# Grouped-query attention and a gated unit on one core: gate with tokens on partitions, and the projection moved behind the next batch's first tiles

## The chip, the cores and the metric

The kernel runs on one core of a Trainium2 chip. The core has five engines that run their own instruction queues in order: TensorE (PE, with weight loads shown apart as PEld), VectorE (DVE), ScalarE (ACT), GpSimd (POOL) and SyncE (SP), which here issues nearly all transfers. The transfers of a core run on 16 DMA engines. The metric is the device time of one execution in microseconds (us). Before the change it is 260.7 us, the median of three runs (259.04 to 261.53).

## The reference

Eight batches of attention with 16 query heads over 4 key and value heads (384 tokens, head size 64), then a gated unit over the 1,024 joined columns. Inputs and output are float32; the kernel works in float16 with float32 sums.

```python
scores = scale * np.matmul(q, k.transpose(0, 1, 3, 2))
attn = np.exp(scores - max); attn = attn / sum
x = (attn @ v), heads joined: (B, 384, 1024)
h = np.maximum(x @ w_in, 0.0)                 # w_in 1024 x 1024
u, v = h[..., :512], h[..., 512:]
v_n = (v - mean(v)) / np.sqrt(var(v) + 1e-06) # over the 512 columns of a token
v_s = np.einsum('ts,bsd->btd', w_spatial, v_n) + b_spatial[None, :, None]
out = (u * v_s) @ w_out                       # w_out 512 x 1024
```

## The kernel before

The order of instructions is written out by hand. One loop of 150 steps `n` makes the program; a batch has 18 steps (`NU`), one for each of its 6 groups `m` (query tile `qt`, head half `j`) times 3 key tiles.

In a step the loop first runs what `at(n, ...)` has put on its list (loads, casts, transposing transfers), then, at even `n`, `scores` for two steps (four matmuls with 64 rows of contraction, and one exponential of 128x1024 on ACT for each step), then `weigh` for a group whose three exponentials came before (12 matmuls of 65 columns, a reciprocal and a product on DVE that write a part of `x16`), then transposes on PE that `turn_at` has put there, and last `run_fill`: as many matmuls of the gated unit as the step is owed, counted in columns. PE runs exactly this order. So attention of one batch and the gated unit of the batch before it are interleaved.

`x16` has the tokens on partitions; the gated unit needs it turned (`xt`, columns on partitions). In batch 0, and for the last third of batch 7, PE does that. Otherwise SP issues transposing transfers, `x_turn`: the first third (`qt` 0) in step 18b+8, the second in step 18b+14, the last in two pieces in steps 18b+17 and 18b+20. k and q of the later batches are turned in the same way, by `k_turn` and `q_turn` (L226 and L233) in steps 10 and 12 of the batch before. Raw k, q and v of a batch are loaded (in step 11 of two batches earlier) and cast on POOL. All of these stand in one queue on SP, in the order of the steps: first x piece, `k_turn`, `q_turn` 0, four loads, `q_turn` 1, second x piece, and so on. At the end of each output tile SP also issues its write to HBM.

`gated_unit(b)` (L306) is a generator that yields the columns of each matmul. `pv` (L314): three token tiles, each 8 matmuls of 512 columns; then relu, mean and variance on DVE. `pu` (L336): four column tiles m of u, transposed (columns on partitions, 384 tokens in the free direction), 8 matmuls of 384 each; relu on ACT. In between, the inverse deviation on ACT, and the normalised `vn` on POOL (L354). `psp` (L366, L369): for each of the four column tiles one matmul that adds the bias to an empty accumulator (a row of ones times a row of bias) and three that mix the tokens; DVE multiplies by u into `gT` (L377). `po` (L384): for each token tile two halves of four matmuls with 512 columns; DVE and ACT copy a half each (L393), SP writes the tile (L397).

The unit of batch b starts in step 18(b+1)+2 and is spread over 18 steps; that of batch 0 starts in step 13. A unit has 43,008 columns, so a step gets 2,389 (2,048 for the first unit, some of which is done early). The accumulators of the unit share three PSUM buffers (`ps_ck`). The rest of batch 7's unit comes after the last attention step, and PE runs it alone.

Of the kernel before, what the change touches and what calls it, by code (L numbers as in the profile page):

```python
# [9 lines left out]
FP32 = mybir.dt.float32  # L10
FP16 = mybir.dt.float16
AF = mybir.ActivationFunctionType
ALU = mybir.AluOpType
# [4 lines left out]
def kernel(  # L18
# [16 lines left out]
    nc = tc.nc  # L35
    P = 128
    B, HQ, S, D = q.shape
# [3 lines left out]
    DH = DFF // 2  # L41
# [14 lines left out]
    att = ctx.enter_context(tc.tile_pool(name="att", bufs=2))  # L56
    moe = ctx.enter_context(tc.tile_pool(name="moe", bufs=2))
    small = ctx.enter_context(tc.tile_pool(name="small", bufs=4))
    ops = ctx.enter_context(tc.tile_pool(name="ops", bufs=4))
    ps_sc = ctx.enter_context(tc.tile_pool(name="ps_sc", bufs=2, space=PSUM))  # L60
    ps_av = ctx.enter_context(tc.tile_pool(name="ps_av", bufs=1, space=PSUM))
    ps_ck = ctx.enter_context(tc.tile_pool(name="ps_ck", bufs=3, space=PSUM))
# [92 lines left out]
    v1 = [cst.tile([P, HKV, NT, VW], FP16, name=f"v1_{i}") for i in range(2)]  # L155
    for i in range(2):
        nc.gpsimd.memset(v1[i][:, :, :, D:VW], 1.0)
    ones_b = cst.tile([P, P], FP16, name="ones_b")
    nc.gpsimd.memset(ones_b, 0.0)
    nc.gpsimd.memset(ones_b[0:1, :], 1.0)  # L160
    nc.gpsimd.memset(ones_b[32:33, :], 1.0)
    bias_b = cst.tile([P, S], FP16, name="bias_b")
    nc.gpsimd.memset(bias_b, 0.0)


    k16s, q16s = {}, {}
# [118 lines left out]
    def x_tile(b):  # L285
        if b not in xts:
            xts[b] = att.tile([P, NT, NB, P], FP16, name=f"xt_{b}", tag="xt")
        return xts[b]
# [13 lines left out]
        )  # L302

    def gated_unit(b):  # L306
        xt = x_tile(b)
        last = b == B - 1
        mv = small.tile([P, NT, 2], FP32, name=f"mv_{b}", tag="mv")
        v_r, v_n = [], []  # L310
        for st in range(NT):
            pv = ps_ck.tile([P, 512], FP32, name=f"pv_{b}_{st}", tag="ck")
            for kt in range(NB):
                nc.tensor.matmul(  # L314
                    pv,
                    xt[:, st, kt],
                    w_in16[:, kt, DH:DFF],
                    start=(kt == 0),
                    stop=(kt == NB - 1),
                )  # L320
                if kt < NB - 1:
                    yield 512
            vr = moe.tile([P, DH], FP32, name=f"vr_{b}_{st}", tag="vr", bufs=4)
            nc.vector.tensor_scalar(vr, pv, 0.0, None, op0=ALU.max)  # L324
            stats = small.tile([P, 6], FP32, name=f"stats_{b}_{st}", tag="stats")
            nc.vector.bn_stats(stats, vr)  # L326
            nc.vector.bn_aggr(mv[:, st, :], stats)
            v_r.append(vr)
            yield 512
        rstd = small.tile([P, NT], FP32, name=f"rstd_{b}", tag="rstd")  # L330
        nmr = small.tile([P, NT], FP32, name=f"nmr_{b}", tag="nmr")
        uT = moe.tile([P, NM, S], FP16, name=f"uT_{b}", tag="uT")
        for m in range(NM):
            pu = ps_ck.tile([P, 512], FP32, name=f"pu_{b}_{m}", tag="ck")
            for kt in range(NB):
                nc.tensor.matmul(  # L336
                    pu[:, 0:S].rearrange("p (t s) -> p t s", t=NT),
                    w_in16[:, kt, m * P : (m + 1) * P],
                    xt[:, :, kt],
                    start=(kt == 0),  # L340
                    stop=(kt == NB - 1),
                )
                yield S
            nc.scalar.activation(uT[:, m, :], pu[:, 0:S], AF.Relu)  # L344
            if m == 0:
                nc.scalar.activation(rstd, mv[:, :, 1], AF.Ln, bias=eps_t)
                nc.scalar.activation(rstd, rstd, AF.Exp, scale=-0.5)
            if m == 1:
                nc.vector.scalar_tensor_tensor(  # L349
                    nmr, mv[:, :, 0], -1.0, rstd, op0=ALU.mult, op1=ALU.mult  # L350
                )
                for st in range(NT):
                    vn = moe.tile([P, DH], FP16, name=f"vn_{b}_{st}", tag="vn", bufs=6)
                    nc.gpsimd.tensor_scalar(  # L354
                        vn,
                        v_r[st],
                        rstd[:, st : st + 1],
                        nmr[:, st : st + 1],
                        op0=ALU.mult,
                        op1=ALU.add,  # L360
                    )
                    v_n.append(vn)
        gT = moe.tile([P, NM, S], FP16, name=f"gT_{b}", tag="gT")
        for m in range(NM):
            psp = ps_ck.tile([P, 512], FP32, name=f"psp_{b}_{m}", tag="ck")
            nc.tensor.matmul(psp[:, 0:S], ones_b, bias_b, start=True, stop=False)  # L366
            yield S
            for st in range(NT):
                nc.tensor.matmul(  # L369
                    psp[:, 0:S],  # L370
                    v_n[st][:, m * P : (m + 1) * P],
                    wsT16[:, st, :],
                    start=False,
                    stop=(st == NT - 1),
                )
                yield S
            nc.vector.tensor_tensor(gT[:, m, :], psp[:, 0:S], uT[:, m, :], ALU.mult)  # L377
        rows = out[b].rearrange("(p t) d -> p t d", t=NT)
        for tt in range(NT):
            osb = ops.tile([P, DM], FP32, name=f"osb_{b}_{tt}", tag="osb")  # L380
            for half in range(2):
                po = ps_ck.tile([P, 512], FP32, name=f"po_{b}_{tt}_{half}", tag="ck")
                for m in range(NM):
                    nc.tensor.matmul(  # L384
                        po,
                        gT[:, m, tt * P : (tt + 1) * P],
                        w_out16[:, m, half * 512 : (half + 1) * 512],
                        start=(m == 0),
                        stop=(m == NM - 1),
                    )  # L390
                    yield 512
                cols = slice(half * 512, (half + 1) * 512)
                (nc.scalar.copy if half else nc.vector.tensor_copy)(osb[:, cols], po)  # L393
                if last:
                    nc.sync.dma_start(rows[:, tt, cols], osb[:, cols])
            if not last:
                nc.sync.dma_start(rows[:, tt, :], osb)  # L397

    HV = NB * 512
    COLS = NT * HV + NM * NB * S + NM * (NT + 1) * S + NT * 2 * NM * 512  # L400


    b32 = cst.tile([1, S], FP32, name="b32")

    def load_b():
        nc.sync.dma_start(b32, moe_b_spatial.rearrange("(a s) -> a s", a=1))

    def prep_spatial():
        lo32 = cst.tile([1, S], FP32, name="lo32")
        bp = b32.rearrange("a (p t) -> a t p", t=NT)  # L410
        hi = bias_b[0:1, :].rearrange("a (t p) -> a t p", t=NT)
        nc.gpsimd.tensor_copy(hi, bp)
        nc.gpsimd.tensor_tensor(lo32.rearrange("a (t p) -> a t p", t=NT), bp, hi, ALU.subtract)
        nc.gpsimd.tensor_copy(bias_b[32:33, :], lo32)

    def load_ws():
        t = cst.tile([P, NT, S], FP32, name="ws32")
# [19 lines left out]
    def at(n, f, *args):  # L437
        todo.setdefault(n, []).append((f, args))
# [64 lines left out]
    at(19, load_q, 2, 1)  # L503
    at(19, load_v, 2)
    at(20, cast_ws)
    at(20, prep_spatial)
    for st in range(NT):
        turn_at(24 + st, ws_transposes, st)
    for c in range(2):
# [22 lines left out]
            elif m > 3:  # L532
                at(s0 + 3 * m + 5, x_turn, b, 2, 4 * (m - 4), 4 * (m - 3))

    fill = []
    owed = 0.0
    total = NU * B

    def run_fill(cols):
        nonlocal owed  # L540
        owed = owed + cols if fill else 0.0
        while fill and owed > 0:
            try:
                owed -= next(fill[0])
            except StopIteration:
                fill.pop(0)

    early = 0
    for n in range(total + 6):
        for f, args in todo.pop(n, []):  # L550
            f(*args)
        if n + 1 < NU:
            scores(n + 1)
        elif n >= NU and n % 2 == 0 and n < total:
            scores(n)
            scores(n + 1)
        for hh in range(2):
            b, r = divmod(n - 3 - hh, NU)
            if n >= 3 + hh and r % 3 == 0 and b < B:
                weigh(b, r // 3, hh)  # L560
        for f, args in turns.pop(n, []):
            f(*args)
        if n == 13:
            fill.append(gated_unit(0))
        if n >= 2 * NU + 2 and (n - 2) % NU == 0 and (n - 2) // NU <= B:
            fill.append(gated_unit((n - 2) // NU - 1))
        if n < NU + 3:
            if 13 <= n and early < 2 * HV:
                c = min(768, 2 * HV - early)
                early += c  # L570
                run_fill(c)
        else:
            run_fill((COLS - (early if n < 2 * NU + 2 else 0)) / (NU if n >= 2 * NU + 2 else NU - 1))
    for g in fill:
        for _ in g:
            pass
    assert not todo and not turns
# [1 line left out]
_INS = ['q', 'k', 'v', 'moe_w_in', 'moe_w_spatial', 'moe_b_spatial', 'moe_w_out']  # L579
# [26 lines left out]
```

## Time and profile before

| what | us |
|---|---|
| median of three runs | 260.7 |
| the profiled execution, its own time | 262.4 |
| its span (first to last instruction) | 260.3 |
| PE busy | 246.5 |
| ACT busy | 169.3 |
| DVE busy | 140.7 |
| POOL busy | 72.8 |
| mean share of the DMA engines, main queue | 72.6% of the span |
| mean granted clock of PE | 0.967 |

The page gives, for each group of equal instructions, the engine, the operation, output and inputs, the count, the busy time, the mean duration of one, and the idle time just before them with what ended it. A matmul's duration is its time in flight, and neighbours overlap. The chain of waits follows the last instruction back to what released it; lines like "87.29 0.54 PE sc L252 x4" in it give start, length and what ran. The list of SP's queue gives the start and the time that SP was held by an instruction; a transfer's landing is counted from its issue. A batch takes 28.5 us in the middle of the run: the first `pv` of the units starts at 65.64, 94.11, 124.02, 152.53, 181.01 and 209.60 us.

### The profile page before, as it was taken

Reading aid. Unit: us, or ns where it says so; the run is one execution under the profiler, and the core shown is the slowest. Engines: PE = TensorE matmul, PEld = TensorE weight load, DVE = VectorE, ACT = ScalarE, POOL = GpSimd, SP = SyncE. Lnnn points to the kernel's source line nnn. Section 1 sums busy time; section 2 is a strip of 40 time slices with the busy share of each in tenths; the row PEclk is TensorE's granted clock in tenths of the full one; section 3 lists DMA queues with packets and bytes.
Section 4 is the critical chain, followed back from the end, with each engine's and each line's share of the span. In section 5 each row is a group of like instructions: output and inputs, shape, how many; then the busy total and the mean of one; then the engine's idle time right before and its main releaser. Section 6 shows DMA issues by size and latency. Waiting matters only on the chain.

```text
span 260.3 us, 5771 instructions
## 1 busy us (share of the span) xinstructions
PE 246.5 (95%) x2339; PEld 126.3 (49%) x2339; DVE 140.7 (54%) x368; ACT 169.3 (65%) x219; POOL 72.8 (28%) x112
## 2 busy tenths in 40 slices
PE   6789889999999999998999999999999999999994
PEld 6445445554455444553455444554455445545551
DVE  3336678355664557274564557274755467364642
ACT  3857556777677776868477776868677776861221
POOL 2455799433003510316003610333021000300110
PEclk9755999999999999999999999999999999999999
DMA  7999798899529991899748991799549350126006
GB/s 189 330 354 353 278 387 263 147 324 224 189 38 197 305 288 52 108 280 209 287 39 195 309 309 33 147 329 232 176 79 134 114 191 14 29 40 241 3 0 242
DMA packets 78827, 49.84 MB, mean 191 GB/s; under 512 B 48081, under 2 KB 72658, under 8 KB 78802
## 3 DMA queue, kind: packets, MB, share of 16 engines
q1 hardware_dynamic: 77762, 49.23, 72.6%
q8 instruction: 18, 0.29, 0.5%
q10 hardware_dynamic: 1040, 0.26, 0.4%
q14 instruction: 7, 0.06, 0.1%
HBM read 25.76 MB, written 12.58 MB: 147 GB/s over the span
## 4 chain that ended last, share of the span: by engine, by line
PE 89%; DVE 5%; ACT 3%; issue 1%; POOL 0%; DVEq 0%; POOLq 0%
PE av L266 16%; PE pu L336 16%; PE pv L314 16%; PE sc L252 15%; PE po L384 15%; PE psp L369 6%; ACT aT L259 2%; PE psp L366 2%; DVE x L278 2%; PE warm L453 1%; DVE qT L224 1%; ACT osb L393 1%; DVE r L276 1%; DVE gT L377 1%; PE qps L217 1%
## 5 line engine op out<-in xcount | busy, mean ns | idle before, releaser
L259 ACT ACTIVATE aT<-sc 128x1024 f16<-128x1024 f32 x144 | 139.9, 1023 | 62.4 <-PE sc L252 62.4
L266 PEld LDWEIGHTS <-aT 128*128 128x128 f16 x1152 | 46.1, 100 | 33.6 <-issue 8.5
L276 DVE RECIPROCAL r<-av 128x4 f32<-128x4 f32 x96 | 17.0, 177 | 73.2 <-PE av L266 73.2
L266 PE MATMUL av<-v,aT 128*128 128x65 f16 x1152 | 54.7, 198 | 1.3 <-DVE x L278 1.0
L252 PE MATMUL sc<-qT,kT 64*128 64x512 f16 x288 | 47.1, 399 | 5.2 <-DVE qT L224 2.7
L354 POOL TENSOR_SCALAR vn<-vr,rstd,nmr 128x512 f16<-128x512 f32 x24 | 18.2, 772 | 115.3 <-DVE nmr L349 93.5
L336 PE MATMUL pu<-xt,w_in 128*128 128x384 f16 x256 | 47.8, 326 | 0.6 <-ACT uT L344 0.6
L384 PE MATMUL po<-w_out,gT 128*128 128x512 f16 x192 | 47.8, 379 | 0.4 <-ACT osb L393 0.3
L314 PE MATMUL pv<-w_in,xt 128*128 128x512 f16 x192 | 47.0, 379 | 0.2 <-DVE osb L393 0.2
L278 DVE TENSOR_TENSOR x<-av,r 128x256 f16<-128x256 f32 x96 | 40.8, 425 | 3.3
L336 PEld LDWEIGHTS <-w_in 128*128 128x128 f16 x256 | 23.1, 98 | 15.9 <-issue 3.4
L189 POOL CAST q<-q 128x768 f16<-128x768 f32 (+1 forms) x32 | 24.8, 802 | 20.0 <-DMA q<-in_q_dram 16.0
L314 PEld LDWEIGHTS <-xt 128*128 128x128 f16 x192 | 16.7, 97 | 17.5 <-issue 2.1
L252 PEld LDWEIGHTS <-kT 64*128 64x128 f16 x288 | 9.1, 95 | 32.7 <-issue 27.0
L384 PEld LDWEIGHTS <-gT 128*128 128x128 f16 x192 | 16.7, 97 | 16.1 <-DVE gT L377 1.7
L377 DVE TENSOR_TENSOR gT<-psp,uT 128x384 f16<-128x384 f32 x32 | 17.7, 557 | 10.5 <-PE psp L369 9.8
L369 PE MATMUL psp<-wsT,vn 128*128 128x384 f16 x96 | 22.2, 326 | 0.0
L393 ACT COPY osb<-po 128x512 f32<-128x512 f32 x24 | 14.2, 590 | 12.1 <-PE po L384 12.1
L324 DVE TENSOR_SCALAR vr<-pv 128x512 f32<-128x512 f32 x24 | 16.6, 692 | 9.6 <-PE pv L314 9.1
L344 ACT ACTIVATE uT<-pu 128x384 f16<-128x384 f32 x32 | 15.7, 493 | 9.3 <-PE pu L336 9.3
L393 DVE COPY osb<-po 128x512 f32<-128x512 f32 x24 | 16.5, 688 | 6.1 <-PE po L384 6.0
L326 DVE BATCH_NORM_STATS2 stats<-vr 128x6 f32<-128x512 f32 x24 | 16.7, 695 | 0.8
(48 smaller groups left out, 106.6 us busy)
## 6 DMA issues: line engine op xcount, KB each, us to landing
q<-in_q_dram SPq DMA_DIRECT2D x14, 768.0 KB, 7.5
out_dram<-osb SPq DMA_DIRECT2D x21, 512.0 KB, 3.5
wi<-in_moe_w_in_dram SPq DMA_DIRECT2D x4, 1024.0 KB, 9.7
v<-in_v_dram SPq DMA_DIRECT2D x8, 384.0 KB, 8.5
k<-in_k_dram SPq DMA_DIRECT2D x7, 384.0 KB, 4.3
wo<-in_moe_w_out_dram SPq DMA_DIRECT2D x2, 1024.0 KB, 5.0
out_dram<-osb SPq DMA_DIRECT2D x6, 256.0 KB, 2.0
q<-in_q_dram SPq DMA_DIRECT2D x2, 512.0 KB, 7.3
```

The lines of the kernel that those rows point to most:

```text
L189: f(q16s[b, j][:, lo:hi, :, hh, :], src[:, hh, lo:hi])
L252: nc.tensor.matmul(sc[:, hh], kTs[b][half, j, t * P : (t + 1) * P], qTs[b, j][half, qt], start=True, stop=True,)
L259: nc.scalar.activation(aTs[b, m][:, t], sc, AF.Exp, scale=scale)
L266: nc.tensor.matmul(av[:, i, :], aTs[b, m][:, t, hh, i * P : (i + 1) * P], v1[b % 2][:, 2 * j + hh, t, 0 : D + 1], start=(t == 0), stop=(t ...
L276: nc.vector.reciprocal(r, av[:, :, D : D + 1])
L278: nc.vector.tensor_tensor(x16s[b][:, qt, blk : blk + 2].rearrange("p k (i d) -> p (k i) d", i=2), av[:, :, 0:D], r.to_broadcast([P, G, D]) ...
L314: nc.tensor.matmul(pv, xt[:, st, kt], w_in16[:, kt, DH:DFF], start=(kt == 0), stop=(kt == NB - 1),)
L336: nc.tensor.matmul(pu[:, 0:S].rearrange("p (t s) -> p t s", t=NT), w_in16[:, kt, m * P : (m + 1) * P], xt[:, :, kt], start=(kt == 0), stop ...
L369: nc.tensor.matmul(psp[:, 0:S], v_n[st][:, m * P : (m + 1) * P], wsT16[:, st, :], start=False, stop=(st == NT - 1),)
L377: nc.vector.tensor_tensor(gT[:, m, :], psp[:, 0:S], uT[:, m, :], ALU.mult)
L384: nc.tensor.matmul(po, gT[:, m, tt * P : (tt + 1) * P], w_out16[:, m, half * 512 : (half + 1) * 512], start=(m == 0), stop=(m == NM - 1),)
L393: (nc.scalar.copy if half else nc.vector.tensor_copy)(osb[:, cols], po)
```

## The change

The gate is computed with tokens on partitions. `u_tile` makes u with tokens on partitions (three tiles of 8 matmuls with 512 columns). `gate` mixes the tokens in three tiles of three matmuls with 512 columns; the bias is then one number per partition, and one DVE operation adds it and multiplies by u. The bias matmuls and their operands go. The gated tile has to be turned before the projection: `g_turn`, one transposing transfer of 12 blocks on SP, for batches 0 to 6; `g_transposes`, 12 transposes on PE with copies by ACT and DVE, for batch 7.

The units become one stream, `stream`: after the gate of batch b come the first two `v_tile`s of batch b+1, and only then the projection of b. The stream starts in step 13 as before with 768 columns a step, up to step 22 in place of 20; from step 23 on, a step gets 2,304 columns (2,332 in the first 18 steps). A unit has 41,472 columns. The buffers of output tiles go from 4 to 3, those of `vr` from 4 to 6.

```diff
-    ops = ctx.enter_context(tc.tile_pool(name="ops", bufs=4))
+    ops = ctx.enter_context(tc.tile_pool(name="ops", bufs=3))
...
-    ones_b = cst.tile([P, P], FP16, name="ones_b")
...
+    bias_c = cst.tile([P, NT], FP32, name="bias_c")
...
-    def gated_unit(b):
...
+    def v_tile(b, st):
...
+        vr = moe.tile([P, DH], FP32, name=f"vr_{b}_{st}", tag="vr", bufs=6)
...
+    def u_tile(b, st):
+        if st == 0:
+            u_s[b] = moe.tile([P, NT, DH], FP16, name=f"u_{b}", tag="u")
+        pu = ps_ck.tile([P, 512], FP32, name=f"pu_{b}_{st}", tag="ck")
+        for kt in range(NB):
+            nc.tensor.matmul(
+                pu,
+                xts[b][:, st, kt],
+                w_in16[:, kt, 0:DH],
+                start=(kt == 0),
+                stop=(kt == NB - 1),
+            )
+            if st == 1 and kt == 3:
+                normal(b)
+            if kt < NB - 1:
+                yield 512
+        nc.scalar.activation(u_s[b][:, st], pu, AF.Relu)
...
+    def gate(b, tt):
+        if tt == 0:
+            g_s[b] = moe.tile([P, NT, DH], FP16, name=f"g_{b}", tag="g")
+        ps = ps_ck.tile([P, 512], FP32, name=f"psp_{b}_{tt}", tag="ck")
+        for st in range(NT):
+            nc.tensor.matmul(
+                ps,
+                wsT16[:, st, tt * P : (tt + 1) * P],
+                v_ns[b][st],
+                start=(st == 0),
+                stop=(st == NT - 1),
+            )
+            if st < NT - 1:
+                yield 512
+        nc.vector.scalar_tensor_tensor(
+            g_s[b][:, tt], ps, bias_c[:, tt : tt + 1], u_s[b][:, tt], op0=ALU.add, op1=ALU.mult
+        )
+        yield 512
+
+    def g_turn(b):
+        gTs[b] = moe.tile([P, NT, NM, P], FP16, name=f"gT_{b}", tag="gT")
+        nc.sync.dma_start(
+            gTs[b].rearrange("p t m s -> p (t m) s"),
+            g_s[b].rearrange("p t f -> p (t f)"),
+            transpose=True,
+        )
+
+    def g_transposes(b, tt):
...
+        for m in range(NM):
+            nc.tensor.transpose(ps[:, m], g_s[b][:, tt, m * P : (m + 1) * P], ident16)
+        nc.scalar.copy(gTs[b][:, tt, 0:2], ps[:, 0:2])
+        nc.vector.tensor_copy(gTs[b][:, tt, 2:4], ps[:, 2:4])
+
+    def project(b, tt):
...
+    def stream():
+        for st in range(2):
+            yield from v_tile(0, st)
+        for b in range(B):
+            yield from v_tile(b, 2)
             for st in range(NT):
+                yield from u_tile(b, st)
+            for tt in range(NT):
+                yield from gate(b, tt)
+            if b + 1 < B:
+                g_turn(b)
+                for st in range(2):
+                    yield from v_tile(b + 1, st)
+            for tt in range(NT):
+                if b + 1 == B:
+                    g_transposes(b, tt)
+                yield from project(b, tt)
 
     HV = NB * 512
-    COLS = NT * HV + NM * NB * S + NM * (NT + 1) * S + NT * 2 * NM * 512
+    COLS = 2 * NT * HV + NT * NT * 512 + NT * 2 * NM * 512
...
     def load_b():
-        nc.sync.dma_start(b32, moe_b_spatial.rearrange("(a s) -> a s", a=1))
...
+        nc.sync.dma_start(bias_c, moe_b_spatial.rearrange("(p t) -> p t", t=NT))
...
-    at(20, prep_spatial)
...
-    fill = []
+    fill = stream()
...
-        if n < NU + 3:
-            if 13 <= n and early < 2 * HV:
+        if n < NU + 5:
+            if n >= 13 and early < 2 * HV:
                 c = min(768, 2 * HV - early)
                 early += c
                 run_fill(c)
         else:
-            run_fill((COLS - (early if n < 2 * NU + 2 else 0)) / (NU if n >= 2 * NU + 2 else NU - 1))
+            run_fill((COLS + (2 * HV - early if n < 2 * NU + 5 else 0)) / NU)
```

## The prediction

> **What bounds the kernel now.** I read the page's busy line and its chain first, then the groups of the gated unit, then SyncE's queue (SPq) with the landing times of its transfers, and last the granted clock by stretches.
>
> ```profile
> PE 246.5 (95%) x2339; PEld 126.3 (49%) x2339; DVE 140.7 (54%) x368; ACT 169.3 (65%) x219; POOL 72.8 (28%) x112
> PE 89%; DVE 5%; ACT 3%; issue 1%; POOL 0%; DVEq 0%; POOLq 0%
> ```
>
> TensorE is the bound: 89% of the chain is matmuls, and no stage has another engine near it. So a removed matmul is worth its streaming time, and a wait in PE's in-order queue is a loss of its whole length. The groups of the gated unit:
>
> ```profile
> L336 PE MATMUL pu<-xt,w_in 128*128 128x384 f16 x256 | 47.8, 326 | 0.6 <-ACT uT L344 0.6
> L384 PE MATMUL po<-w_out,gT 128*128 128x512 f16 x192 | 47.8, 379 | 0.4 <-ACT osb L393 0.3
> L369 PE MATMUL psp<-wsT,vn 128*128 128x384 f16 x96 | 22.2, 326 | 0.0
> L366 PE MATMUL psp<-bias_b,ones_b 128*128 128x384 f16 x32 | 10.4, 325 | 0.0
> ```
>
> The means (326, 379 ns) are the time that one matmul is in flight; they overlap. The pace is in the chain: in the tail 24 pv take 5.34 us (222 ns each) and 32 pu 5.20 us (162.5 ns each); in the middle five pv take 1.08 us (216 ns).
>
> Then SyncE's queue in batch 2's steps, in order of start (start, duration, what):
>
> ```profile
> 75.67 1.23 SPq L298 DMA_TRANSPOSE xt<-x  x1
> 77.00 1.24 SPq L227 DMA_TRANSPOSE kT<-k  x1
> 78.33 1.45 SPq L234 DMA_TRANSPOSE qT<-q  x1
> 79.83 1.46 SPq L80 DMA_DIRECT2D k<-in_k_dram  x1
> 81.35 1.20 SPq L86 DMA_DIRECT2D q<-in_q_dram  x2
> 82.59 1.83 SPq L83 DMA_DIRECT2D v<-in_v_dram  x1
> 84.46 5.03 SPq L234 DMA_TRANSPOSE qT<-q  x1
> 89.59 1.34 SPq L298 DMA_TRANSPOSE xt<-x  x1
> ```
>
> The first line turns the first third of batch 2's x (call it X0), the last one the second third (X1). X1's data were ready by about 84 us (the DVE write of x before it ends at 83.8), but SP got to it at 89.59: the turn of q before it sits 5.03 us in SP behind four loads of 2.3 MB. Its landing:
>
> ```profile
> L298 SPq DMA_TRANSPOSE xt<-x x1: 1344/1344/1344, 89.6 to 89.6; - x1
> DMA to landing us min/median/max: 3.4/3.4/3.4
> ```
>
> So X1 lands at 93.0. Today that is in time, as pv of batch 2 starts at 94.1. Batch 6, in whose steps nothing is left to load, has the same instructions without the blockage:
>
> ```profile
> 191.04 1.23 SPq L298 DMA_TRANSPOSE xt<-x  x1
> 192.37 1.24 SPq L227 DMA_TRANSPOSE kT<-k  x1
> 193.71 3.34 SPq L234 DMA_TRANSPOSE qT<-q  x2
> 199.34 1.23 SPq L298 DMA_TRANSPOSE xt<-x  x1
> ```
>
> **What the change removes.** 32 bias matmuls at 162.5 ns: 5.2 us. The columns of pv, pu, psp and po stay the same (pu 32x384 = 24x512 a batch, psp 12x384 = 9x512), so the wider shapes move nothing but some 0.2 us of per-matmul overhead, which I leave out. On DVE 32 products of 557 ns (17.8 us) become 24 of 128x512, between the 692 ns of vr and 557x512/384 = 743 ns: 17 us, equal. On ACT 32 relus of 493 ns become 24 of about 600. POOL loses four memsets and the bias preparation (689 + 1019 + 496 ns near 35 us); it has 28% busy and nothing waits for it there. The bias now comes as one load of 128x3 in place of 1x384, at the same place in SP's queue and far ahead of its first use: nothing. All of this is nothing on the chain. The third buffer less in `ops` costs nothing: an output tile lands in 3.5 us and is needed again a batch (28 us) later.
>
> **The start.** The steps 21 and 22 fill 768 columns instead of 2,048, 1.07 us of matmuls put off. If ACT's exponentials (1.02 us a step) then set the pace, up to 1.07 us are lost; I take 0.3.
>
> **The tail.** Twelve transposes on PE at about 0.06 us (the trace's qps take 0.25 us per four) add 0.7. Before: from psp's first (248.43) to po's last, 8 us with one wait of 0.56. After, from gate's start: three psp groups end at 1.95; the product of the third ends on DVE near 3.0, and only behind it DVE copies its half of the first turned tile (292 ns), so po starts near 3.4 instead of 2.2: 1.2 lost. The second and third tile each wait for ACT, which copies the last po (590 ns) and then its half of the turned tile (372 ns), with about 0.05 to 0.2 between: 1.0 less 0.25 for the transposes already counted, twice 0.75. With 0.7 of transposes and 0.5 of today's wait gone: 1.2 + 1.5 + 0.7 - 0.5 = +2.9. Bounds 0 and 4.
>
> So without new waits the span is 260.3 - 5.2 + 2.9 + 0.3 = 258.3.
>
> **What moves: `v_tile(b+1, 0)` and `(b+1, 1)` are now ahead of the projection of b.** In the new order of PE the first matmul of `v_tile(b,1)` stands directly in front of the scores of step 18b+16; before, it came some six steps later. It waits for X1's landing. Put on the times of before (start of those scores less one matmul of 0.22), against X1's landing (issue plus its own landing time):
>
> batch 1: PE there at 59.0, X1 lands 60.29 + 3.4 = 63.7: late by 4.7
> batch 2: 87.1, 89.59 + 3.4 = 93.0: 5.9
> batch 3: 115.6, 119.78 + 4.5 = 124.3: 8.7
> batch 4: 145.5, 148.04 + 4.7 = 152.7: 7.3
> batch 5: 174.0, 175.89 + 5.4 = 181.3: 7.3
> batch 6: 202.6, 199.34 + 4.2 = 203.5: 0.9
> batch 7: 231.0, 227.81 + 3.1 = 230.9: 0
>
> Batches 1 to 5 sum to 33.9. Three corrections: eight steps of 85 columns less (0.29 us, batches 2 to 5) +1.1; batch 1's steps get 284 columns more, -0.95; X0 goes out one matmul earlier (the DVE statistics of the last v tile, 1.57 us, stand before it), four times -0.2. That leaves 33.3. A stall delays X0 of the next batch too, and with it the loads and X1, so the lateness returns each batch and is not worked off: from X0's issue to X1's landing the queue needs 17.3 to 19.7 us, PE needs 11 to 12 (14 in batch 1). Behind the waiting weight load stand, on PE, the next two steps' scores and weighings and all later fill, so ACT and DVE run dry as well and nothing covers the wait.
>
> **The queue's new instruction.** `g_turn(b)`, seven times twelve blocks, like q's turn: 1.45 us on SP when unhindered, landing 3.7 to 4.9 after its start. It stands behind X1. Behind it wait the third x pieces and the outputs, which have 11 us or more. PE wants it 8 matmuls, a score group and a weighing after X1's landing: 8x0.216 + 0.54 + 0.49 = 2.8. It lands 1.4 + 4.9 - 4.2 = 2.1 after X1, up to 3.5 with a slow issue: 0 to 0.7 each. I take 1 for all, and 1 for batches 6 and 7.
>
> **The clock.** PE would now stand still for 5 to 9 us. What the grant does is seen early in the trace (stretch, length, then PE busy and the other engines, granted clock, DMA share, GB/s):
>
> ```profile
> 7.00:13.00 6.00, 4.53 (x43) 2.52 (x41) 1.89 (x7) 5.46 (x6) 3.18 (x5) 0.70 1.11 331
> 13.00:20.00 7.00, 5.72 (x56) 3.12 (x56) 2.50 (x8) 3.96 (x5) 3.26 (x6) 0.50 1.08 353
> 20.00:26.00 6.00, 5.36 (x53) 3.00 (x51) 3.94 (x12) 4.18 (x6) 3.69 (x5) 0.50 1.08 354
> ```
>
> The grant fell to half near 9.4 us after three us in which the chain ran through ACT's first exponentials (6.75 to 9.65), and came back near 26.4, after PE had run without a gap from 22.9 on: 3.4 us at half pace, 1.7 us lost. Behind each stall PE has dense work, so I take 1.7 for each of five: 8.5. Bounds: 0, and 17 us at half pace, 8.5 for each.
> The Trainium skill ("TensorE: Matmul & The Clock Gate", Part 1) speaks against this change: an idle window of about 3.4 us halves the clock and a busy window restores it, the window running freely. An estimate from it is 1.7 to 3.4 us per stall, a sum up to 8.5 us above mine; the trace's row agrees in kind but fell with PE busy about two thirds of that time.
>
> **Sum.** 258.3 + 33.3 + 1 + 1 + 8.5 = 302.1 for the span. The profiled execution took 262.4, 2.1 more than its span, and lies 1.7 above the median 260.7; so on the median's scale 0.4 comes on top: 302.5. With stalls of 5.3 to 8.6 each and 0 to 3.4 for the clock this case runs from 286 to 321.
>
> **Rivals.**
> Only SP's own issue time counts (16%): the 5.03 us is not repeated, because the loads drain while PE stands. SP still needs 84.46 - 75.67 + 1.45 + 0.1 = 10.3 from X0 to X1, landing 3.4 to 4.2 later: 2.3 to 3.1 late, too short to move the clock. 258.3 + 5x2.7 + 1 + 0.4 = 273. Against it: the DMA engines' share is 0.92 to 1.06 from X0 to X1 in batches 1 to 5, and none of that work depends on PE.
> The second turn is in time (7%): X0 to X1's landing in under 11.4 us, the point from which PE never waits. Batch 6 comes near it (12.5), but it has no loads; five batches say 17.3 or more. Then only the saving is left, 258.3 + 0.4 = 258.7, 0.8% below the median.
> The clock stays down as it did early, 17 us per stall (5%): 258.3 + 33.3 + 2 + 42.5 + 0.4 = 336.5. Against it: after each stall PE has filling matmuls without gaps, which the early stretch had not.
>
> **The numbers.** My forecast has 72% and 302.5. The range takes the second case in and leaves out the last two and the edges: 272 to 322. One per cent is about what a measurement of this kernel tells from no change; slower by more 0.92, within it 0.05, faster 0.03, both from the third case.
>
> **What will show it.** Waits of PE's weight loads of pv (L307) on the landing of xt, about 5 to 8 us, once a batch, five times, some 33 us in all; SP still sitting 4 to 6 us in q's second turn ahead of X1; the granted clock at half in a stretch after each; psp in 72 matmuls at 216 ns; three waits of about 1 us in the tail. If X1 goes out within 10 us of X0, the first rival holds; if PE waits for gT and not xt, I have the wrong transfer; if the clock stays full, 8.5 us of mine are wrong.

## The result, and the profile after

The changed kernel takes 302.43 us (median of four runs, 300.81 to 303.83), the kernel before 260.24 beside it (259.04 to 261.53): 1.163 times as long, 95% interval 1.155 to 1.172. The profiled execution of the changed kernel took 300.81 us, its span is 298.9, the mean granted clock 0.931. Medians and ranges are over all executions of a kernel, but the ratios leave out those more than 1.5% above its fastest: one each in e2 (1300.71 us, cause not known), e5, e6 and e10 and two in e8, among them the profiled ones of e5, e6 and e8.

First the page's busy line and the chain's shares by engine:

```profile
PE 250.7 (84%) x2231; PEld 114.7 (38%) x2231; DVE 141.2 (47%) x363; ACT 170.2 (57%) x214; POOL 70.3 (24%) x105
PE 50%; SPq 19%; DMA 18%; ACT 4%; POOL 3%; issue 3%; DVE 2%; POOLq 0%; DVEq 0%; ACTq 0%
```

PE's share of the span fell from 95% to 84%, its share of the chain from 89% to 50%. In its place stand SyncE's queue and transfers, which had no part in the chain of before. PE's waits say which transfers (what it waited for: us in total, times, longest):

```profile
PE pv L307 <- DMA xt<-x: 31.1, 6, 6.5
PE po L410 <- ACT gT L400: 1.9, 3, 0.7
```

Five of the six waits for x, 30.9 us together, are those of batches 1 to 5; the sixth (0.2) is in batch 7.

Then SyncE's queue in batch 2's steps (start, duration, what), to be laid beside the same stretch of before:

```profile
80.17 1.23 SPq L293 DMA_TRANSPOSE xt<-x  x1
81.51 1.24 SPq L222 DMA_TRANSPOSE kT<-k  x1
82.84 1.47 SPq L229 DMA_TRANSPOSE qT<-q  x1
84.37 0.88 SPq L80 DMA_DIRECT2D k<-in_k_dram  x1
85.30 1.15 SPq L86 DMA_DIRECT2D q<-in_q_dram  x2
86.50 1.81 SPq L83 DMA_DIRECT2D v<-in_v_dram  x1
88.35 6.02 SPq L229 DMA_TRANSPOSE qT<-q  x1
94.47 1.44 SPq L293 DMA_TRANSPOSE xt<-x  x1
96.01 1.46 SPq L388 DMA_TRANSPOSE gT<-g  x1
```

The order and the hold are those of before: X0 at the top, the second turn of q held for 6.02 us behind the four loads, X1 behind it. The chain follows PE's wait back to exactly this place (start, duration, what):

```profile
88.35 6.02 SPq L229
...
94.47 3.43 DMA xt<-x
...
97.95 0.61 PE pv L307
```

What this costs on the engines shows in the timeline of the same moment (the brackets give the idle time before, and what ended it):

```profile
97.95 0.61 PE L307 MATMUL pv<-w_in,xt 128*128 128x512 f16 x1 [6.19 <-DMA xt<-x]
99.14 1.94 ACT L254 ACTIVATE aT<-sc 128x1024 f16<-128x1024 f32 x2 [7.87 <-PE sc L247]
```

PE stood still for 6.19 us, and the scores queued behind the waiting matmul kept ACT idle for 7.87: nothing covers the wait. The last view is the stretch behind each of the five waits (from:to, length, PE busy, PEld, DVE, ACT, POOL, granted clock, DMA share, GB/s):

```profile
61.00:66.40 5.40, 5.40 (x25) 2.05 (x26) 0.63 (x3) 1.94 (x2) 0.00 (x0) 0.50 0.31 63
97.95:104.00 6.05, 6.05 (x26) 2.05 (x26) 1.21 (x3) 1.94 (x2) 0.00 (x0) 0.50 0.33 63
135.52:141.50 5.98, 5.98 (x26) 2.05 (x26) 1.14 (x3) 1.94 (x2) 0.00 (x0) 0.50 0.31 60
172.77:175.70 2.93, 2.93 (x19) 1.17 (x20) 0.51 (x2) 1.74 (x2) 0.00 (x0) 0.50 0.41 76
208.25:213.20 4.95, 4.95 (x24) 1.94 (x25) 0.61 (x2) 1.94 (x2) 0.00 (x0) 0.50 0.39 75
```

PE is busy in every microsecond of these and has half the clock: 25.3 us in all, of which half, 12.65, is lost. A reader who looks at busy time alone misses this: it counts as PE at work.

So the span's 38.6 us more can be laid out by the starts of X0, which both kernels have. From X0 of batch 1 to that of batch 6 (45.44 to 191.04 before, 41.40 to 227.40 after) the run is 40.4 longer. The terms give 40.3: 30.9 of waits and 12.65 of clock, less 3.25 for five batches' bias matmuls. Batch 6 takes 28.5 in both (0.1 less after). From X0 of batch 7 to the end it is 43.0 in place of 40.7, and the start, up to X0 of batch 1, is 4.0 shorter: 40.4 - 0.1 + 2.3 - 4.0 is 38.6.

### The profile page after: what moved, and what is told of

Read it like the earlier page. It is cut to its first block, busy times and chain, and to the rows that moved or that the text cites. A ratio compares the mean times of both kernels' runs of the same rounds, so it can differ in the third digit from the quotient of the medians.

```text
span 298.9 us, 5561 instructions
## 1 busy us (share of the span) xinstructions
PE 250.7 (84%) x2231; PEld 114.7 (38%) x2231; DVE 141.2 (47%) x363; ACT 170.2 (57%) x214; POOL 70.3 (24%) x105
## 4 chain that ended last, share of the span: by engine, by line
PE 50%; SPq 19%; DMA 18%; ACT 4%; POOL 3%; issue 3%; DVE 2%; POOLq 0%; DVEq 0%; ACTq 0%
PE po L410 14%; PE pv L307 11%; SPq L229 9%; PE av L261 8%; DMA xt<-x 8%; PE sc L247 8%; PE pu L329 7%; DMA q<-in_q_dram 4%; DMA k<-in_k_dram 3%; DMA wi<-in_moe_w_in_dram 3%; SPq L83 3%; SPq L86 3%; ACT aT L254 2%; POOL vn L357 2%; SPq L80 1%
## 5 line engine op out<-in xcount | busy, mean ns | idle before, releaser
L307 PE MATMUL pv<-w_in,xt 128*128 128x512 f16 x192 | 57.4, 423 | 31.2 <-DMA xt<-x 31.1
L261 PEld LDWEIGHTS <-aT 128*128 128x128 f16 x1152 | 45.0, 99 | 38.3 <-issue 15.0
L410 PE MATMUL po<-w_out,gT 128*128 128x512 f16 x192 | 49.6, 385 | 1.9 <-ACT gT L400 1.9
L329 PE MATMUL pu<-w_in,xt 128*128 128x512 f16 x192 | 47.5, 379 | 0.0
L273 DVE TENSOR_TENSOR x<-av,r 128x256 f16<-128x256 f32 x96 | 40.7, 424 | 3.3
L307 PEld LDWEIGHTS <-xt 128*128 128x128 f16 x192 | 17.9, 105 | 54.3 <-DMA xt<-x 35.0
L329 PEld LDWEIGHTS <-xt 128*128 128x128 f16 x192 | 16.9, 97 | 18.5 <-issue 2.5
L173 POOL CAST v<-v 128x768 f16<-128x768 f32 x8 | 6.6, 829 | 56.9 <-PE av L261 50.1
L381 DVE SCALAR_TENSOR_TENSOR g<-psp,bias_c,u 128x512 f16<-128x512 f32 x24 | 17.3, 745 | 4.5 <-PE psp L372 4.5
L372 PE MATMUL psp<-vn,wsT 128*128 128x512 f16 x72 | 18.5, 379 | 0.6 <-POOL vn L357 0.6
L340 ACT ACTIVATE u<-pu 128x512 f16<-128x512 f32 x24 | 14.4, 601 | 5.9 <-PE pu L329 5.9
```

The costliest lines, as they stand in the source:

```text
L261: nc.tensor.matmul(av[:, i, :], aTs[b, m][:, t, hh, i * P : (i + 1) * P], v1[b % 2][:, 2 * j + hh, t, 0 : D + 1], start=(t == 0), stop=(t ...
L273: nc.vector.tensor_tensor(x16s[b][:, qt, blk : blk + 2].rearrange("p k (i d) -> p (k i) d", i=2), av[:, :, 0:D], r.to_broadcast([P, G, D]) ...
L307: nc.tensor.matmul(pv, xts[b][:, st, kt], w_in16[:, kt, DH:DFF], start=(kt == 0), stop=(kt == NB - 1),)
L329: nc.tensor.matmul(pu, xts[b][:, st, kt], w_in16[:, kt, 0:DH], start=(kt == 0), stop=(kt == NB - 1),)
L372: nc.tensor.matmul(ps, wsT16[:, st, tt * P : (tt + 1) * P], v_ns[b][st], start=(st == 0), stop=(st == NT - 1),)
L410: nc.tensor.matmul(po, gTs[b][:, tt, m], w_out16[:, m, half * 512 : (half + 1) * 512], start=(m == 0), stop=(m == NM - 1),)
```

## The experiments

The theory is that of the forecast: X1 lands late since SyncE's transposing transfers are held behind the loads' backlog, PE waits for it once in each of batches 1 to 5, and the clock is halved behind each wait. Its rivals: the place in SyncE's queue and its issue time are what counts; the new transfer of the gated tile is to blame; the half clock is a matter of chance and not of the wait.

**e1_qturn_behind.** q's second turn goes behind X1.

```diff
-            at(w0 + 12, q_turn, b, 1)
+            at(w0 + 16, q_turn, b, 1)
```

> The second turn of q is issued four steps later, behind the second x piece and the gated tile's turn; nothing else moves. If only SP's place in line is late (the hold belongs to q's turn), the x piece goes out when its data are ready, about 10 us after the first piece, lands 3.4 us later and PE waits 1 to 3 us a batch: 265 to 275 us. If the cause is the backlog of the loads on the DMA engines, the x piece is held in SP in place of q's turn and lands only about 1.5 us earlier than now: the five waits shrink from 6.3 to about 4.5 us and the time is 288 to 296 us. I expect the second.

292.76 us (292.54 to 295.31), 1.132 times before (1.123 to 1.140). In the same stretch of SyncE's queue (start, duration, what), X1 now stands directly behind the loads:

```profile
84.99 1.89 SPq L83 DMA_DIRECT2D v<-in_v_dram  x1
87.11 4.22 SPq L293 DMA_TRANSPOSE xt<-x  x1
91.43 2.59 SPq L388 DMA_TRANSPOSE gT<-g  x1
94.08 1.51 SPq L229 DMA_TRANSPOSE qT<-q  x1
```

X1 itself is held, 4.22 us in place of 1.44, and lands 7.6 us after its issue in place of 3.4. q's turn, now last, takes 1.51. In the other four batches X1 is held for 3.4 to 3.5 us, and in all five the gated tile's turn behind it takes 2.4 to 3.1. So the hold goes to the transposing transfer that comes first behind the loads, with a part of it to the next. PE's waits for x are 24.4 us in place of 31.1, five weight-load waits of 4.9 to 5.8. A rival that counts SyncE's own issue time (273 us) is not what happens.

**e2_loads_moved.** The loads of k, q and v go out ten steps later, behind the x pieces of the batch, with their casts and turns behind them.

```diff
-                at(w0 - NU + 11, load_k, b)
...
+                at(w0 + 3, load_k, b)
...
-            at(w0 + 6, cast_k, b, pool)
...
+            c0 = w0 + 10 if b > 2 else w0 + 6
+            at(c0, cast_k, b, pool)
...
-            at(w0 + 10, k_turn, b)
-            at(w0 + 10, q_turn, b, 0)
-            at(w0 + 12, q_turn, b, 1)
+            at(w0 + 12, k_turn, b)
+            at(w0 + 12, q_turn, b, 0)
+            at(w0 + 16, q_turn, b, 1)
```

> The four loads of batches 3 to 7 go from ahead of the second x piece to just behind the last x piece of the batch before (with their casts behind the normalised tiles, the turn of k two steps later, and the second turn of q behind the second x piece). If the loads' backlog is what makes the second x piece late, no batch waits more than about 1 us, as batches 6 and 7 show now, the clock stays full, and the time is 256 to 263 us. If PE's wait has another cause (the amount of transposing transfers, or the place of the v tiles in PE's order by itself), waits of several us stay and the time is above 285 us.

268.09 us (three of the four executions 267.43 to 268.75), 1.033 times before (1.026 to 1.039): 34 us of the 42 come back. The turns of k and q were moved as well as the loads; e1, which has the second turn of q behind X1 as here, had brought 10 of them, so 25 are left for the loads, their casts and the two steps by which the turn of k and the first of q are later. But 256 to 263 was expected. PE's waits, and the chain around 140 us (start, duration, what), name the rest; the last view is SyncE's queue at that place:

```profile
PE pv L307 <- DMA xt<-x: 8.0, 7, 1.9
```

```profile
140.38 0.75 DVE g L381
...
141.25 0.22 DVE x L273
...
142.52 3.60 DMA xt<-x
...
146.16 0.39 PE pv L307
```

```profile
139.47 1.29 SPq L222 DMA_TRANSPOSE kT<-k  x1
141.01 1.41 SPq L229 DMA_TRANSPOSE qT<-q  x1
142.52 1.61 SPq L293 DMA_TRANSPOSE xt<-x  x1
```

With the backlog gone, X1 goes out as soon as the k and q turns ahead of it allow (q's turn starts on SyncE at 141.01 and takes 1.41), and x's last write waits on DVE behind the gate's product (0.75). The transfer takes 3.6, and the new order of the units gives it 2.3. The forecast's sum without waits, 258.3, plus these 8.0 is 266.3; the span is 265.6, with the granted clock at 1.0 throughout. That sum still holds the early half clock of the profiled execution of before (260.3), which e2 has not; executions of before at full clock have spans of 256.7 to 259.4, so up to 3 us of e2 stay unassigned. The waits, none above 1.9 us, did not move the clock here.

**e4_gate_turned_on_pe.** All batches turn the gated tile on PE; the transfer `g_turn` goes.

```diff
-                g_turn(b)
...
-                if b + 1 == B:
-                    g_transposes(b, tt)
+                g_transposes(b, tt)
```

> The gated tile is turned on PE in every batch, so the new transfer is gone from SP's queue; the two v tiles stay ahead of the projection. If the second x piece is the cause, the five waits of about 6.3 us stay, and 84 transposes more (7 x 12 at 0.056 to 0.1 us, 5 to 8 us) with some waits for their copies come on top: 303 to 318 us. If the new transfer was to blame, the time falls below 285 us.

318.87 us (318.30 to 319.64), 1.229 (1.223 to 1.236), 0.9 above what was expected at most. PE's waits:

```profile
PE pv L307 <- DMA xt<-x: 29.9, 5, 7.0
PE po L410 <- ACT gT L400: 15.0, 23, 0.7
```

The wait for x stays, and one for ACT's copies comes on top, 0.65 us for each of 23 tiles. The transfer of the gated tile is not what makes x late.

**e5_busy_wait.** PE gets 24 matmuls whose result nobody reads, in front of the one that waits for X1, in batches 1 to 5.

```diff
+                    if st == 1 and b + 1 < 6:
+                        wm = ps_ck.tile([P, 512], FP32, name=f"warm_{b}", tag="ck")
+                        for _ in range(24):
+                            nc.tensor.matmul(wm, ident16, w_in16[:, 0, 0:512], start=True, stop=True)
```

> 24 matmuls of 512 columns (24 x 0.216 = 5.2 us) that nobody reads are put in PE's order right before the second v tile of batches 1 to 5, where PE waits 6.2 to 6.5 us now; they fit into the wait. If the lowered clock after the waits costs what the trace of after says (25 us of work at half pace, 12.6 us lost), the clock stays full and the time falls to 288 to 293 us. If the clock costs nothing because the work behind the wait is not bound by PE, it stays at 301 to 304 us.

293.18 us (290.62 to 295.34), 1.127 (1.117 to 1.137): 9 us less than the changed kernel by the medians, 10 by the ratios, though work was added. The dummies fill most of the wait (6.2 us of waiting are left) and do not shorten it. The stretches around the first two waits (columns as above):

```profile
60.00:70.00 10.00, 9.60 (x77) 4.23 (x76) 3.87 (x10) 4.09 (x5) 0.91 (x2) 1.00 0.53 107
100.00:110.00 10.00, 9.98 (x91) 4.46 (x90) 6.06 (x15) 7.39 (x9) 0.83 (x1) 1.00 0.47 132
```

Where the changed kernel had 0.50, the clock is full. Behind four of the five waits it stays so; behind the fourth, of 1.89 us, it is half for 3.4 us. So the half clock comes from PE standing still, and it is worth 9 to 10 us; the 12.65 read off the trace is one execution's.

**e3_second_v_behind.** Only `v_tile(b+1, 0)` stays ahead of the projection.

```diff
-                for st in range(2):
-                    yield from v_tile(b + 1, st)
+                yield from v_tile(b + 1, 0)
...
+            if b + 1 < B:
+                yield from v_tile(b + 1, 1)
```

> Only the first v tile of the next batch stays ahead of the projection, the second goes behind it; the turned gate still comes by transfer. The second x piece is then wanted 24 matmuls later and is in time. If the whole queue of SP is late, the gated tile's turn, which stands behind that piece, is now what PE waits for: it lands about 19 us after the first x piece went out, the projection wants it after about 11.5: 7 to 8 us in batches 1 to 5, about 2 in the others, and the time is 303 to 315 us. If only the early need of the second x piece was wrong, the time falls to 258 to 266 us.

311.96 us (310.52 to 314.81), 1.200 (1.192 to 1.209). PE's wait has a new name, and more of it:

```profile
PE po L410 <- DMA gT<-g: 43.2, 7, 8.6
```

X1 and the gated tile are neighbours in SyncE's queue (96.65 and 98.18 us in batch 2) behind the same hold of 5.47 us; what needs either of them first waits. Seen with e4, the order on PE decides only which of the two is named.

**e6_gate_alone.** Gate and bias as changed, but the projection directly behind the gate as before, with the gated tile turned on PE in all batches.

```diff
+            for tt in range(NT):
+                g_transposes(b, tt)
+                yield from project(b, tt)
             if b + 1 < B:
-                g_turn(b)
                 for st in range(2):
                     yield from v_tile(b + 1, st)
-            for tt in range(NT):
-                if b + 1 == B:
-                    g_transposes(b, tt)
-                yield from project(b, tt)
```

> The gate with tokens on partitions alone: each projection follows its gate directly, the gated tile is turned on PE in every batch, no v tile goes ahead and no new transfer is issued. If the long waits come from the move and SP's queue, no wait of more than 1 to 2 us is left and the clock stays full. Saved are 5.2 us of bias matmuls, added 96 transposes (0.056 to 0.1 us each, 5 to 10 us) and in each batch waits for the copies, between 0 (hidden by attention's matmuls) and 2.7 us (as in the tail): 260 to 285 us; I take 268.

287.49 us (285.57 to 291.59), 1.100 (1.093 to 1.107), above the expected bound of 285. The copies are not hidden by the attention:

```profile
PE po L410 <- ACT gT L400: 23.9, 24, 1.8
```

260.3 less 5.2 for the bias and plus 23.9 of waits is 279.0; the span is 289.7. The other 10.7 hold the 96 transposes themselves (5 to 10 us by the expectation) and the clock. Two stretches (columns as above), the first just behind a wait of 1.76 us that began at 85.1:

```profile
87.44:90.84 3.40, 3.40 (x23) 1.77 (x21) 1.27 (x3) 0.04 (x1) 2.57 (x4) 0.54 1.22 218
90.84:96.00 5.16, 3.70 (x33) 1.60 (x30) 1.88 (x5) 3.61 (x6) 0.36 (x1) 1.00 0.74 206
```

The clock was near half for 3.4 us, then full, although PE idled 28% of the second window. The trace has four such dips of 3.4 us each, 6.8 us lost in all. They come and go with the execution: two others, at a granted clock of 0.999 and 1.0, have spans of 284.7 and 283.7. The early half clock of before, which counts the other way, is missing here; how the 10.7 divide was not measured.

**e7_stream_later.** SyncE's queue as changed, but the stream of units fills with 768 columns a step for five steps more, and so runs up to five steps behind.

```diff
-        if n < NU + 5:
-            if n >= 13 and early < 2 * HV:
-                c = min(768, 2 * HV - early)
+        if n < NU + 10:
+            if n >= 13:
+                c = 768
...
-            run_fill((COLS + (2 * HV - early if n < 2 * NU + 5 else 0)) / NU)
+            run_fill((COLS + (2 * HV - early if n < 2 * NU + 10 else 0)) / NU)
```

> Nothing of SP's queue is touched: only the stream of the gated units is put five steps later against attention (768 columns a step up to step 27, the batch's share from step 28 on). The second v tile then comes about 8 us later after the first x piece has gone out, at 19 us where the landing needs 17.3 to 18.3. If the wait is a race between that piece's fixed way through SP's queue and PE's place in its order, it is gone with the clock's loss and the gated tile's transfer still lands in time: 256 to 262 us. If PE's stream and the queue move together, or another transfer takes the place of the late one, waits of several us stay: above 275 us.

270.08 us (268.91 to 272.07), 1.037 (1.032 to 1.041), between the two expectations. PE has no wait for x any more; it has others:

```profile
PE sc L247 <- DMA qT<-q: 3.4, 4, 1.8
...
PE po L410 <- DMA gT<-g: 1.9, 3, 1.1
```

The chain of this run goes from the evacuation of the projection on ACT to the store of the output on SyncE, the turns of k and q queued behind it, the loads, and the transfer of qT (start, duration, what):

```profile
101.86 0.59 ACT osb L420
...
102.48 0.33 SPq L426
...
111.72 8.21 DMA qT<-q
```

The later stream pushed the outputs, which wait for their data in SyncE's queue, in front of the next batch's turns. So the lateness of x against PE is what cost the time, but a shift of PE's work moves SyncE's queue as well.

**e8_later_and_tail.** e7, and in the last batch the copies of a turned tile get a group of matmuls to hide behind: gate 0, gate 1, turn 0, gate 2, turn 1, project 0, turn 2, project 1, project 2.

> The same, and in the last batch each turn of a gated tile on PE is put one group of matmuls ahead of its projection (turn 0 before gate 2, turn 1 before projection 0, turn 2 before projection 1), so that the copies lie beside matmuls. The three waits of the tail (0.5, 0.7 and 0.7 us on PE, more in its weight loads) should go: 1.5 to 2.5 us less than the run beside it, 254 to 260 us. If the copies on ACT and DVE are late all the same, no difference.

269.18 us (266.30 to 270.82), 1.028 (1.023 to 1.034). PE's wait for the copies is gone from the list. That is 0.9 us less than e7 by the medians and 2.1 by the ratios, where 1.5 to 2.5 was expected; the intervals overlap, so the size is not settled. The 254 to 260 in all was missed, as e7 itself was slower than expected.

**e9_loads_and_one_step, e10_loads_and_two_steps.** The loads of e2, the tail of e8, and the stream of e7 with `NU + 6` and `NU + 7` in place of its `NU + 10`.

> The loads moved as in the run with 268 us, the stream of the units one step (1.6 us) later, and the last batch's turns put one group ahead. That run still waited 8.0 us for the second x piece, 1.8 to 2.4 us on PE's weight loads in each of four batches, since the DVE product of 745 ns and the turns of k and q stand ahead of the piece. One step should hide most of it: 266 span less about 6 less about 2 of tail, 257 to 262 us. If the saved matmuls are lost elsewhere (PE waiting for DVE in each batch), it stays at 264 us or above.

> The same with the stream two steps (3.2 us) later: the wait for the x piece is gone in every batch: 255 to 260 us, below the kernel before. If later outputs now hold up the turns of k and q in SP's queue (as with five steps, 270 us), it is above the run with one step.

e9: 256.71 us (253.69 to 257.38), 0.983 of before (0.978 to 0.988), just under the expected 257 to 262. e10: 256.07 us (254.48 to 258.50), 0.981 (0.975 to 0.986), within 255 to 260. The two can't be told apart. Neither waits for a transfer of x, q or the gated tile. The busy line of e10:

```profile
PE 238.3 (94%) x2231; PEld 112.9 (45%) x2231; DVE 139.9 (55%) x363; ACT 170.3 (67%) x214; POOL 69.7 (28%) x105
```

PE's share is back at 94%, with 8 us less of PE's busy time than in the profiled execution of before. Most of that is clock by estimate: the half clock lasted 17.1 us there and 3.4 here. The saving is seen in the times: executions at a granted clock of 1.0 took 253.69 to 257.19 us in e9 and e10, and 259.22 to 260.05 in the kernel before beside them. So with its transfers in time the changed kernel is 1.7 to 1.9% faster than the one before (1.2 to 2.5 by the intervals). How much of this is the gate and how much the moved loads and the regrouped tail was not separated, as the kernel before was not run with its loads moved. Its PE waits for no transfer, which suggests that little is to be had there.

## Why the prediction was right

The forecast was 302.5 us and 302.43 was measured, by the mechanism named: PE's in-order queue stands at the second v tile until X1 has landed. That the sum agrees to 0.1 is luck, as its terms are off by up to 4 us in both directions.

- **The five waits: 33.3 forecast, 30.9 measured** as PE's own idle time (33.4 by the weight loads, 6.3 to 7.0 each). The reading behind it, that the hold repeats since none of the loads' work depends on PE, is shown by the queue (4.6 to 6.0 us in every batch) and by e1 and e2. The raw lateness by batch (4.7 to 8.7) was worse than the sum: each wait sets X0 of the next batch, so they settle near one value.
- **The clock: 8.5 forecast, 12.65 in the profiled execution, 9 to 10 by e5.** The half clock began during each wait and lasted 6.8 or 10.2 us, of which 2.9 to 6.1 lay behind the wait, where 3.4 was taken from one early stretch. The Trainium skill ("TensorE: Matmul & The Clock Gate", Part 1) has the clock halved by an idle window of about 3.4 us and restored by a busy one of that length, the window running freely. The estimate from it was 1.7 to 3.4 lost per wait, and 1.5 to 3.0 is what the five stretches show. The same rule does not cover e6, where a wait of 1.76 us was followed by half a clock.
- **The transfer of the gated tile: 1 forecast, 0 measured.** PE never waits for it in batches 0 to 6. It goes out 1.5 us behind X1 and so hides in the wait for X1. It has its price once x is in time: 1.9 us in e7.
- **Batches 6 and 7: 1 forecast, 0.6 and 0.2 measured** (on PE's weight load and on PE). Batch 6 shows the same 28.5 us in both kernels, so the 0.65 saved with the bias was given back. The chain there, shown below the list, has no load in it: the gate's product on DVE, the transfer of X1, the wait of pv. X1 is also what e2 still waited for. In batches 1 to 5 it was hidden under the larger one; the forecast had priced it for batches 6 and 7 only.
- **The tail: +2.9 forecast less 0.65 of bias, 2.3 measured** from the gate's first matmul to the projection's last (10.45 us in place of 8.19). The three waits are there, with 1.9 us in all. That it is 2.3 from X0 of batch 7 on as well is chance: two units' bias is saved in that stretch, and other waits, 0.66 us for x on DVE among them, take it back.
- **The start: +0.3 forecast, 4.0 shorter in the profiled execution.** This term is the furthest off. The early stretch of half clock, which the forecast took as given, is absent in this execution (mean 1.00 up to X0 of batch 1, 0.81 before). The change did not remove it: e5, with the same first steps, has 0.61 from 8 to 30 us. It comes and goes between executions, and the profiled run was the fastest of its four, 1.6 below their median. Executions of before at full clock are 0.9 to 3.6 us shorter than its profiled one; whether the clock is all of the 4.0 was not separated.
- **The saving of 5.2** is not seen as such in the changed kernel, but the stretch of batches 1 to 5 only adds up with it, and e9 and e10 end below the kernel before. The products on DVE took 745 ns (692 to 743 was the bound) and, as forecast, do not bound the span, but by standing ahead of x on DVE they belong to the remaining wait of e2.
- **One number of the working was wrong.** A step of the first unit got (43,008 - 6,144) / 17 = 2,168 columns before the change, not 2,048, as eight early steps take 768 each. So steps 21 and 22 put off 1.17 us of matmuls instead of 1.07, and batch 1's steps gain 164 columns each instead of 284, which makes the sum of the waits 0.4 larger.

The chain into batch 6's wait (start, duration, what):

```profile
234.46 0.75 DVE g L381
...
235.78 3.21 DMA xt<-x
...
239.04 0.39 PE pv L307
```

PE's timeline in the tail, with the idle time before each tile's first matmul in brackets:

```profile
287.29 1.90 PE L410 MATMUL po<-w_out,gT 128*128 128x512 f16 x8 [0.46 <-ACT gT L400]
290.14 1.90 PE L410 MATMUL po<-w_out,gT 128*128 128x512 f16 x8 [0.73 <-ACT gT L400]
293.00 1.90 PE L410 MATMUL po<-w_out,gT 128*128 128x512 f16 x8 [0.73 <-ACT gT L400]
```

The rival with SyncE's issue time alone (273) failed on the first line it was to be known by: X1 goes out 14.3 us after X0 in batch 2, not within 10. The clock that stays down for 17 us did not come either.

## What to carry to other kernels

Before work is moved earlier in an in-order queue, lay the time at which it will now be reached against the landing of each transfer it reads, and take the landing from the same stage of the trace: a transfer that is in time by a microsecond today is a stall tomorrow. Where a transfer sits long in its queue, find what stands ahead of it in the DMA engines; moving the loads, with the turns around them, paid 34 us here, moving one turn within the queue only 10. A PE stall also has to be priced with the clock behind it, and a few matmuls that nobody needs show how large that part is.

## What the runs showed of the hardware

- The transposing transfer that comes first behind some 2.3 MB of loads is held on SyncE: q's second turn for 4.6 to 6.0 us, X1 in its place (e1) for 3.4 to 4.2, against 1.2 to 1.7 for nearly all others of the changed kernel. In e1 X1's landing took 6.6 to 7.9 us in place of 3.4 as well. Loads are not the only cause: in batch 6 of the changed kernel, with no load in the queue, q's second turn was held for 3.47 us directly behind three other transposing transfers.
- The granted clock did not follow the length of a wait alone: it fell with the waits of 6 to 7 us each time, behind one of 1.76 us in e6, and not at all behind those of up to 1.9 us in e2. The traces show what else counts: the clock changed on a grid of 3.41 us. Every half-clock stretch inside a run lasted one to five times that (3.41 to 17.07 us), and the four of e6 begin 34.1 us, ten grid steps, apart.
- From 30 us on and up to the last 10 us of a run, each fall came behind a grid step in which PE was busy for 49% of the time or less, and none came behind a fuller one. In e6 the wait of 1.76 us lay within one step (83.66 to 87.07, PE busy 1.65 us); in e2 one of 1.87 us was split over two (82.49 to 85.91 with 1.95 busy, 85.91 to 89.32 with 3.01). The rule is not sharp: two steps, with 47% (e2, from 113.21) and 48% (e6, from 220.19), were not followed by half clock. What exactly the chip counts stays open.
- The half clock of the first 30 us comes and goes between executions of kernels with the same first steps (0.61 in e5, 1.00 in the changed kernel). In nine of the twelve traces it began behind a step with PE busy for 59 to 63%, so busy time alone does not mark it. One profiled execution is no measure of the start.
